# Pooled attention and a four-expert layer on one core: keys and values fetched as two accumulating half transfers

## The chip, the core and the metric

The kernel runs on one core of a Trainium2 chip. The core has a matrix engine (TensorE, in profiles PE, with its weight loads as PEld), three engines for element-wise work (VectorE = DVE, ScalarE = ACT, GpSimd = POOL), a queue engine (SyncE = SP), and 16 DMA engines that move data between the main memory and the on-chip memory. The metric is the device time of one execution in microseconds. The kernel before takes 524.53 us (median of three; 523.56 to 525.8).

## What is computed

Eight batches of eight heads, 576 queries of 64 numbers each. Keys and values are averaged over groups of 8 rows (72 pooled rows remain), then comes ordinary softmax attention, and its output passes through four experts, each two matrix products with a relu between, weighted per token.

```python
B, H, S, D = 8, 8, 576, 64; pool = 8
k_p = k.reshape(B, H, 72, 8, D).mean(axis=3)
v_p = v.reshape(B, H, 72, 8, D).mean(axis=3)
attn = softmax(q @ k_p.T / sqrt(D))
x = (attn @ v_p) as (4608, 512)
p = domain_probs / domain_probs.sum(-1)
for e in range(4):                     # w1[e]: 512x1024, w2[e]: 1024x512
    out += p[:, e] * (relu(x @ w1[e]) @ w2[e])
```

All inputs are float32 in main memory; GpSimd's transfers turn them into bfloat16 on their way.

## The kernel before

Work goes in chunks c of 512 tokens: c = 0 to 7 are the first 512 tokens of each batch, c = 8 the 64 last tokens of all batches together. A chunk has four steps, one for each expert e. In step (c, e), TensorE computes the first product of (c, e) and, mixed in, the second product of the step before; mixed in further is the attention of batch c + 1. The program places the small pieces by hand: each step has 16 numbered points, and `attention(c)` says at which pair of points of chunk c (n = 0 to 31) what is placed. The engines run their instructions in exactly this order.

The matrix products use a scheme with seven products of half-size blocks instead of eight. It needs sums and differences of blocks ("forms") of the weights and of the activations, made once for the weights:

```python
def combine_w1(e, engine=nc.vector):          # 4 operations 128x1024, bf16, in w1_bf
    ...
        lambda: add(out=w[:, S1], in0=w[:, A21], in1=w[:, A22]),
        ...                                   # S2, S4, S3
def combine_w2(e, engine=nc.vector):          # 4 operations 128x1024, into w2_t and w2_bf
    ...
def sums_of(c, e):                            # 4 operations 128x1024 of the activations (L701 to L704)
    ...
def relu_sum(out, ps, r):                     # VectorE drains a PSUM bank (L686)
    nc.vector._custom_dve(TENSOR_ADD_SAT, out=out, in0=ps[:], in1=r[:], s0=BIG, s1=0.0)
```

Where they are placed (`forms_due` is a queue from which each slot of a step takes one):

```python
if s == 1:
    forms_due.extend(nothing + combine_w1(2))         # nothing = four empty slots
elif s == 2:
    forms_due.extend(combine_w1(3))
elif s == 4:
    forms_due.extend(nothing[:2] + combine_w1(1) + combine_x(1))
elif s == 5:
    forms_due.extend(nothing[:3] + combine_w2(SPLIT[0]))
    forms_due.extend(combine_w2(SPLIT[1], nc.gpsimd) + combine_w1(0, nc.gpsimd))
```

Keys and values are loaded whole, 72 partitions of 8 heads x 8 rows x 64, and folded by VectorE: 8 rows to 4 (`first`), 4 to 2 and 2 to 1 (`rest`). Keys are written twice, side by side, and transposed by a DMA; values go to `vps` and are used as they are.

```python
def load_kv(b, src, nm):
    if b in (1, 2) and nm == "vraw":
        raw = w2_t[0:SP]...                            # borrowed room
    else:
        raw = rawpool.tile([SP, H, POOL, D], BF16, name="raw")[:]   # one buffer
    nc.gpsimd.dma_start(out=raw, in_=src[b].rearrange("h (j r) d -> j h r d", r=POOL))

def fold_parts(nm, b, hs, last):                       # hs: half of the heads
    def first():
        raw = raws[(nm, b)]
        nc.vector.tensor_add(out=raw[:, hs, 0:4, :], in0=raw[:, hs, 0:4, :], in1=raw[:, hs, 4:8, :])
    def rest():
        raw = raws[(nm, b)]
        nc.vector.tensor_add(out=raw[:, hs, 0:2, :], in0=raw[:, hs, 0:2, :], in1=raw[:, hs, 2:4, :])
        for out in last(hs):
            nc.vector.tensor_add(out=out, in0=raw[:, hs, 0, :], in1=raw[:, hs, 1, :])
    return [first, rest]

def loads_wait(b):                                     # GpSimd waits for the transposed keys
    nc.gpsimd.tensor_copy(out=mark[:], in_=state[("kpT", b)][0:1, 0, 0:1])
```

The order of the attention pieces in chunk c (b = c + 1):

```python
    if c == 1:
        keyed = 1
        add(0, lambda: queries(b))                     # DMA transpose of the queries
        for n, part in enumerate(key_parts(b)):
            add(n // 2, part)
    else:
        keyed = 1
        for n, part in enumerate(key_parts(b)[2:]):
            add(n, part)
    scored, valued, mixed = 7, 8 if c > 1 else 6, 11
    add(keyed, lambda: keys(b), lambda: loads_wait(b)) # DMA transpose of the keys; mark
    if c > 1:
        add(keyed + 1, lambda: load_v(b))
    if b + 1 < B:
        add(keyed + 1, lambda: (load_q(b + 1), load_q_rem(b + 1)))
    for pair in range(NPAIR):
        add(scored + pair, lambda pair=pair: scores(b, pair))
    for n, part in enumerate(value_parts(b)):
        add(valued + n, part)
    if b + 1 < B:
        add(valued + 4, lambda: queries(b + 1), lambda: load_k(b + 1))
        for n, part in enumerate(key_parts(b + 1)[:2]):
            add(30 + n, part)
    for r in range(NR):
        add(mixed + r, lambda r=r: context(b, r))      # attention x values on TensorE
        add(mixed + 1 + r, lambda r=r: turn(b, r))
```

In chunk 0 the plan `second_attention` does the same for batch 1, and issues keys, queries and values of batch 2 at its points 44, 51 and 66.

Of the kernel before, what the change touches and what calls it, by code (L numbers as in the profile page):

```python
# [11 lines left out]
ALU = mybir.AluOpType  # L12
AX = mybir.AxisListType
BF16 = mybir.dt.bfloat16
# [4 lines left out]
def kernel(  # L19
# [10 lines left out]
    nc = tc.nc  # L30
# [5 lines left out]
    POOL = 8  # L36
# [38 lines left out]
    w2_t = wpool.tile([P, len(SPLIT), 3, FCH // 2, TH], BF16, name="w2_t")  # L75
    h_s = wpool.tile([P, 3, FCH // 2, TH], BF16, name="h_s")

    raws = {}
    q_rems = {}

# [1 line left out]
    halves = [slice(i * H // 2, (i + 1) * H // 2) for i in range(2)]  # L82

    def load_kv(b, src, nm):
        if b in (1, 2) and nm == "vraw":
            raw = w2_t[0:SP].rearrange("p a b f d -> p (a b f d)")[:, 0:H * POOL * D].rearrange(
                "p (h r d) -> p h r d", h=H, r=POOL
            )
        else:
            raw = rawpool.tile([SP, H, POOL, D], BF16, name="raw")[:]  # L90
        nc.gpsimd.dma_start(
            out=raw, in_=src[b].rearrange("h (j r) d -> j h r d", r=POOL)
        )
        raws[(nm, b)] = raw

    def load_first(src, nm, hs):
        if nm not in raws:
# [34 lines left out]
    def load_k(b):  # L132
        load_kv(b, k, "kraw")

    def load_v(b):
        load_kv(b, v, "vraw")
# [57 lines left out]
    def fold_keys(b, hs):  # L194
        raw = raws[("kraw", b)]
        fold(raw, hs)
        for dup in range(2):
            nc.vector.tensor_add(out=kp[0:SP, hs, dup, :], in0=raw[:, hs, 0, :],
                                 in1=raw[:, hs, 1, :])

    def fold_parts(nm, b, hs, last):

        def first():
            raw = raws[(nm, b)]
            nc.vector.tensor_add(out=raw[:, hs, 0:4, :], in0=raw[:, hs, 0:4, :],  # L205
                                 in1=raw[:, hs, 4:8, :])

        def rest():
            raw = raws[(nm, b)]
            nc.vector.tensor_add(out=raw[:, hs, 0:2, :], in0=raw[:, hs, 0:2, :],  # L210
                                 in1=raw[:, hs, 2:4, :])
            for out in last(hs):
                nc.vector.tensor_add(out=out, in0=raw[:, hs, 0, :], in1=raw[:, hs, 1, :])

        return [first, rest]

    def key_parts(b):
        return [part for hs in halves for part in fold_parts(
            "kraw", b, hs, lambda hs: [kp[0:SP, hs, dup, :] for dup in range(2)])]
# [5 lines left out]
    def keys(b):  # L225
        state[("kpT", b)] = apool.tile([P, H, SPP], BF16, name="kpT", bufs=3)
        nc.sync.dma_start_transpose(
            out=state[("kpT", b)][:], in_=kp[:].rearrange("j h u d -> j (h u d)")
        )
# [13 lines left out]
    def queries(b):  # L243
        state[("qT", b)] = apool.tile([P, H, 2, P], BF16, name="qT", bufs=1)
        nc.sync.dma_start_transpose(
            out=state[("qT", b)][:].rearrange("c h r p -> c (h r) p"),
            in_=raws[("q", b)][:].rearrange("p h r d -> p (h r d)"),
        )
# [254 lines left out]
    def second_attention():  # L503

        lo, hi = halves

        return {
            42: [lambda: fold_keys(1, lo)],
            44: [lambda: fold_keys(1, hi), lambda: load_k(2)],
            47: [second_keys],  # L510
            50: [lambda: second_queries(0)],
            51: [lambda: second_queries(1), lambda: load_q(2), lambda: load_q_rem(2)],
            53: [lambda: scores(1, 0)],
            55: [lambda: scores(1, 1)],
            56: [lambda: fold_values(1, lo)],
            57: [lambda: scores(1, 2)],
            58: [lambda: fold_values(1, hi)],
            59: [lambda: scores(1, 3)],
            60: [lambda: context(1, 0), lambda: turn(1, 0)],
            61: [lambda: context(1, 1), lambda: turn(1, 1)],  # L520
            62: [lambda: context(1, 2), lambda: turn(1, 2)],
            63: [lambda: context(1, 3), lambda: turn(1, 3)],
            66: [lambda: load_v(2)],
        }

    def attention(c):

        lo, hi = halves
        b = c + 1
        plan = {}  # L530

        def add(n, *what):
            plan.setdefault(n, []).extend(what)

        if c % 2:
            i = c // 2
            add(18, lambda: rem_queries(i))
            add(23, lambda: rem_scores(i))
            add(26, lambda: rem_context(i))
            add(27, lambda: rem_turn(i))  # L540
        if b == B:
            for part in forms_of(B):
                add(31, part)
            return plan
        if c == 1:
            keyed = 1
            add(0, lambda: queries(b))
            for n, part in enumerate(key_parts(b)):
                add(n // 2, part)
        else:  # L550
            keyed = 1
            for n, part in enumerate(key_parts(b)[2:]):
                add(n, part)
        scored, valued, mixed = 7, 8 if c > 1 else 6, 11
        add(keyed, lambda: keys(b), lambda: loads_wait(b))
        if c > 1:
            add(keyed + 1, lambda: load_v(b))
        if b + 1 < B:
            add(keyed + 1, lambda: (load_q(b + 1), load_q_rem(b + 1)))
        for pair in range(NPAIR):  # L560
            add(scored + pair, lambda pair=pair: scores(b, pair))
        for n, part in enumerate(value_parts(b)):
            add(valued + n, part)
        if b + 1 < B:
            add(valued + 4, lambda: queries(b + 1), lambda: load_k(b + 1))
            for n, part in enumerate(key_parts(b + 1)[:2]):
                add(30 + n, part)
        for r in range(NR):
            add(mixed + r, lambda r=r: context(b, r))
            add(mixed + 1 + r, lambda r=r: turn(b, r))  # L570
        for n, part in enumerate(forms_of(b)):
            add((20, 21, 28, 29)[n], part)
        return plan
# [274 lines left out]
    with tc.manual_schedule(engines={ENG.PE, ENG.DVE, ENG.Activation, ENG.Pool, ENG.SP}):  # L848
# [52 lines left out]
        for s in range(len(steps) + 1):  # L901
            live = s < len(steps)
            if live:
                c, e = steps[s]
                if e == 0:
                    plan = second_attention() if c == 0 else {}
                    if 0 < c < B:
                        plan = {at + 2 * n + 1: what for n, what in attention(c).items()}
                    for n, what in plan.items():
                        placed.setdefault(n, []).extend(what)  # L910

            def between(j, n):
                point()
                if s > 0:
                    down(*steps[s - 1], j, n)
                slot()

            nothing = [lambda: None] * 4
            if s == 1:
                forms_due.extend(nothing + combine_w1(2))  # L920
            elif s == 2:
                forms_due.extend(combine_w1(3))
            elif s == 4:
                forms_due.extend(nothing[:2] + combine_w1(1) + combine_x(1))
            elif s == 5:
                forms_due.extend(nothing[:3] + combine_w2(SPLIT[0]))
                forms_due.extend(combine_w2(SPLIT[1], nc.gpsimd) + combine_w1(0, nc.gpsimd))
            for j in range(2):
                if not live:
                    for n in range(4):  # L930
                        between(j, n)
                elif s == 0:
                    for i in range(4):
                        up_half(j, i)
                        if j == 0 and i in (1, 2):
                            turn_here(0, i + 1)
                        if j == 0 and i == 2:
                            norm_probs()
                            for part in combine_x(0):
                                part()  # L940
                        between(j, i)
                elif s == 1:
                    for n in range(4):
                        between(j, n)
                    for n in range(4):
                        up_plain(c, e, [4 * j + n])
                elif s == E:
                    for n in range(4):
                        between(j, n)
                        if j:  # L950
                            up_plain(c, e, [2 * n, 2 * n + 1])
                elif splits(*steps[s - 1]):
                    up_down(c, e, j, *steps[s - 1])
                else:
                    up_seven(c, e, j, lambda n: between(j, n))
# [30 lines left out]
```

The softmax here doesn't subtract the row's maximum and nothing guards it: scores larger than these inputs give would overflow.

## Time and profile before

| | busy, us | share of 523.6 us |
|---|---|---|
| TensorE matmuls | 504.0 | 96% |
| TensorE weight loads | 363.5 | 69% |
| VectorE | 355.4 | 68% |
| ScalarE | 267.5 | 51% |
| GpSimd | 67.5 | 13% |
| DMA queue of GpSimd (inputs) | 22.63 MB | 31.0% of 16 engines |
| DMA queue of SyncE (output, transposes) | 18.29 MB | 18.7% of 16 engines |

The DMA engines are full for the first 70 us, when all weights come in, and on average about half busy or less afterwards (a share of 0.46 from 114 to 210 us). A matmul lasts longer than the distance between two of them (0.27 us against 0.11 us for 256 columns), so TensorE's busy share hides nothing but also says little; waits are read from the time between starts. In timeline lines the columns are start, duration, engine, source line, operation, what it writes and reads, count, and in brackets how long the engine was idle before it and what ended that. Two lines of transfers:

```profile
raw<-in_k_dram POOLq DMA_DIRECT2D x7, 576.0 KB, 11.4
raw<-in_v_dram POOLq DMA_DIRECT2D x5, 576.0 KB, 8.1
```

They give the count, the bytes as they arrive, and the median time from issue to landing.

### The profile page before, as it was taken

To read this page: it belongs to the slowest core of one execution; us is meant where nothing else is said; L and a number is where in the kernel's file an instruction comes from. 1 tells how busy PE (TensorE), PEld (TensorE's weight loads), DVE (VectorE), ACT (ScalarE), POOL (GpSimd) and SP (SyncE) were. 2 spreads that over 40 slices of the span, in tenths; PEclk is the share of its full clock that TensorE was granted. 3 is DMA by queue.
4 is the path that set the end of the run, shared out by engine and by line. 5 is a ranking of instruction groups with operands and counts; after the bars stand their busy time and mean duration, and the time that the engine had idled before them with its cause. 6 is when DMAs were issued, how large, how long until landed. Compare 5 with 4: busy or idle time off the path is not lost.

```text
span 523.6 us, 10155 instructions
## 1 busy us (share of the span) xinstructions
PE 504.0 (96%) x4171; PEld 363.5 (69%) x4171; DVE 355.4 (68%) x649; ACT 267.5 (51%) x467; POOL 67.5 (13%) x80
## 2 busy tenths in 40 slices
PE   8898989969999999999999999999999999999996
PEld 4745644558757876688668866886588768866883
DVE  2434787897857884878677876787677546764674
ACT  3653434636465545565465546653655446544650
POOL 8362102860020002000100020000000000000000
PEclk9999999999999999999999999999999999999999
DMA  9999999510199207920696059403510110011003
GB/s 133 207 206 206 199 149 179 107 30 1 24 169 107 25 0 142 145 36 11 106 143 65 2 94 157 70 11 57 94 32 0 41 52 1 11 42 40 1 1 80
DMA packets 75133, 41.56 MB, mean 79 GB/s; under 512 B 44480, under 2 KB 70464, under 8 KB 75088
## 3 DMA queue, kind: packets, MB, share of 16 engines
q0 software_dynamic: 33744, 22.63, 31.0%
q1 hardware_dynamic: 41344, 18.29, 18.7%
q8 instruction: 32, 0.52, 0.4%
q14 instruction: 13, 0.11, 0.1%
HBM read 45.16 MB, written 9.44 MB: 104 GB/s over the span
## 4 chain that ended last, share of the span: by engine, by line
PE 71%; DVE 13%; DMA 10%; POOL 2%; issue 2%; ACT 1%; POOLq 0%; ACTq 0%; SPq 0%; DVEq 0%
PE g_ps L638 30%; PE o_ps L817 19%; PE u_ps L755 16%; DMA w_bf<-in_moe_w_dram 5%; DMA raw<-in_v_dram 3%; DVE H_sb L686 3%; DVE acc L761 3%; DMA kpT<-kp 2%; PE h_ps L656 1%; PE two L262 1%; PE two L385 1%; POOL w_bf L142 1%; DVE h_s L701 1%; DVE x_tok L367 1%; DVE H_sb L702 1%
## 5 line engine op out<-in xcount | busy, mean ns | idle before, releaser
L638 PEld LDWEIGHTS <-w_bf 128*128 128x128 bf16 x1848 | 176.1, 98 | 49.5 <-issue 10.7
L817 PE MATMUL o_ps<-w_bf,H_sb 128*128 128x512 bf16 x640 | 161.5, 379 | 0.2 <-DMA w_bf<-in_moe_w_dram 0.2
L682 ACT COPY r<-g_ps 128x512 f32<-128x512 f32 x166 | 97.4, 586 | 106.3 <-PE g_ps L638 102.4
L638 PE MATMUL g_ps<-xf,w_bf 128*128 128x256 bf16 x1056 | 148.4, 272 | 2.8 <-DVE H_sb L686 1.8
L686 DVE CUSTOM_DVE_ANT_0 H_sb<-g_ps,r 128x512 bf16<-128x512 f32 x166 | 113.9, 687 | 48.1 <-ACT r L682 33.3
L761 DVE SCALAR_TENSOR_TENSOR acc<-u_ps,p_all,acc 128x512 f32<-128x512 f32 (+1 forms) x128 | 78.0, 612 | 43.8 <-ACT u_ps L781 43.1
L638 PE MATMUL g_ps<-xT,w_bf 128*128 128x256 bf16 x696 | 99.9, 273 | 2.0 <-DVE H_sb L686 2.0
L817 PEld LDWEIGHTS <-H_sb 128*128 128x128 bf16 x640 | 62.5, 98 | 46.1 <-issue 0.4
L689 ACT ACTIVATE H_sb<-g_ps 128x512 bf16<-128x512 f32 x98 | 58.4, 596 | 29.7 <-PE g_ps L638 29.7
L755 PEld LDWEIGHTS <-H_sb 128*128 128x128 bf16 x512 | 49.4, 98 | 8.2 <-DVE H_sb L702 2.4
L755 PE MATMUL u_ps<-w_bf,H_sb 128*128 128x256 bf16 x384 | 52.4, 273 | 1.1 <-DVE H_sb L702 0.9
L755 PEld LDWEIGHTS <-h_s 128*128 128x128 bf16 x384 | 37.5, 98 | 6.1 <-DVE h_s L703 1.8
L831 DVE SCALAR_TENSOR_TENSOR acc<-o_ps,p_all,acc 128x512 f32<-128x512 f32 x44 | 32.7, 746 | 11.3 <-PE o_ps L817 11.3
L755 PE MATMUL u_ps<-w_t,h_s 128*128 128x256 bf16 x256 | 38.4, 273 | 1.5 <-DVE h_s L703 1.5
L266 ACT ACTIVATE expT<-two 72x1024 bf16<-72x1024 f32 x28 | 28.6, 1020 | 13.4 <-PE two L262 13.4
L767 ACT COPY g_ps<-g_ps 128x512 f32<-128x512 f32 x32 | 18.3, 572 | 27.9 <-PE g_ps L638 27.9
L828 ACT ACTIVATE acc<-o_ps,p_all 128x512 f32<-128x512 f32 x36 | 24.8, 690 | 7.0 <-PE o_ps L817 7.0
L234 POOL COPY mark<-kpT 1x1 bf16<-1x1 bf16 x6 | 1.3, 218 | 205.9 <-DMA kpT<-kp 205.9
L781 ACT COPY u_ps<-u_ps 128x256 f32<-128x256 f32 x32 | 11.4, 357 | 26.7 <-PE u_ps L755 26.7
L205 DVE TENSOR_TENSOR raw<-raw 72x1024 bf16<-72x1024 bf16 x22 | 15.0, 681 | 13.5 <-DMA raw<-in_v_dram 13.5
L367 DVE TENSOR_TENSOR x_tok<-two,inv 128x512 bf16<-128x512 f32 x32 | 22.1, 691 | 1.1
L385 PEld LDWEIGHTS <-expT 72*128 72x128 bf16 x256 | 12.0, 98 | 12.4 <-DVE x_tok L367 4.8
(113 smaller groups left out, 377.2 us busy)
## 6 DMA issues: line engine op xcount, KB each, us to landing
out_dram<-acc SPq DMA_DIRECT2D x32, 256.0 KB, 2.9
w_bf<-in_moe_w_dram POOLq DMA_DIRECT2D x16, 256.0 KB, 9.7
w_bf<-in_moe_w_dram POOLq DMA_DIRECT2D x4, 1024.0 KB, 16.9
raw<-in_k_dram POOLq DMA_DIRECT2D x7, 576.0 KB, 11.4
q_sb<-in_q_dram POOLq DMA_DIRECT2D x7, 512.0 KB, 11.9
raw<-in_v_dram POOLq DMA_DIRECT2D x5, 576.0 KB, 8.1
w_t<-in_v_dram POOLq DMA_DIRECT2D x2, 576.0 KB, 13.2
out_dram<-acc SPq DMA_DIRECT2D x8, 128.0 KB, 2.3
```

The lines of the kernel that those rows point to most:

```text
L266: nc.scalar.activation(out=state[("expT", b)][:, 2 * pair:2 * pair + 2].rearrange("j h r s p -> j s (h r) p"), in_=two[0:SP].rearrange("j ...
L367: nc.vector.tensor_tensor(out=x_tok[:], in0=c_ps[:, :, :, 0:D], in1=inv[:].unsqueeze(3).to_broadcast([P, 2, NPAIR, D]), op=ALU.mult,)
L638: nc.tensor.matmul(bank[:, t, :], lhsT=w1_bf[:, e, block, kc, lo:lo + P], rhs=x[:, kc, :], start=(first and t == 0 and kc == 0), stop=(t = ...
L682: nc.scalar.copy(out=r[:], in_=ps[:])
L686: nc.vector._custom_dve(TENSOR_ADD_SAT, out=out, in0=ps[:], in1=r[:], s0=BIG, s1=0.0)
L689: nc.scalar.activation(out=out, in_=ps[:], func=ACT.Relu)
L755: nc.tensor.matmul(out, lhsT=lhs[0][:, lhs[1] + f, lhs[2]], rhs=rhs[0][:, rhs[1] + f, rhs[2]], start=(start and f == 0), stop=(f == FCH // ...
L761: nc.vector.scalar_tensor_tensor(out=acc, in0=ps, scalar=prob, in1=acc, op0=ALU.mult, op1=ALU.add,)
L767: nc.scalar.copy(out=s[:], in_=g[:])
L817: nc.tensor.matmul(sums[r][:], lhsT=hidden[(c, e)][:, fc, r * P:(r + 1) * P], rhs=w2_bf[:, e, fc, :], start=(fc == 0), stop=(fc == FCH - 1),)
L828: nc.scalar.activation(out=accs[(c, r)][:], in_=o_ps[:], func=ACT.Copy, scale=prob)
L831: nc.vector.scalar_tensor_tensor(out=dst, in0=o_ps[:], scalar=prob, in1=dst, op0=ALU.mult, op1=ALU.add,)
```

## The change

Keys and values of batches 2 to 7 come as two transfers each. The first brings rows 0 to 3 of every group of 8; the second brings rows 4 to 7 and adds them in flight to what the first wrote. VectorE's `first` is then not needed. Each goes to its own half of one buffer `raw_kv`, so keys and values can be fetched together; batch 1 is still fetched whole, over both halves. The second transfer must wait for the first. The order of pieces follows: in chunk c both halves of keys and values of batch c + 2 are issued at n = 17 and 19. For batch 2 the keys' halves are at points 44 and 47 of chunk 0 and the values' halves at 66. The forms of w1[3] come four slots later, and those of w1[0] go from GpSimd to VectorE. The aim is less work for VectorE and earlier loads.

```diff
+    raw_kv = rawpool.tile([SP, 2, H, POOL // 2, D], BF16, name="raw_kv")
...
+    def load_half(b, src, nm, half):
+        raws[(nm, b)] = raw_kv[:, 0 if nm == "kraw" else 1]
+        lo = half * POOL // 2
+        nc.gpsimd.dma_start(
+            out=raws[(nm, b)],
+            in_=src[b].rearrange("h (j r) d -> j h r d", r=POOL)[:, :, lo:lo + POOL // 2],
+            accum_op=ALU.add if half else ALU.bypass,
+        )
+    def load_later(b, half):
+        load_half(b, k, "kraw", half)
+        load_half(b, v, "vraw", half)
...
     def fold_parts(nm, b, hs, last):
-        def first():
-            ...
-        return [first, rest]
+        return [rest]
...                                                    # second_attention
-            44: [lambda: fold_keys(1, hi), lambda: load_k(2)],
-            47: [second_keys],
+            44: [lambda: fold_keys(1, hi), lambda: load_half(2, k, "kraw", 0)],
+            47: [second_keys, lambda: load_half(2, k, "kraw", 1)],
...
-            66: [lambda: load_v(2)],
+            66: [lambda: load_half(2, v, "vraw", 0), lambda: load_half(2, v, "vraw", 1)],
...                                                    # attention(c)
         if c == 1:
-            keyed = 1
-            add(0, lambda: queries(b))
-            for n, part in enumerate(key_parts(b)):
-                add(n // 2, part)
+            add(0, lambda: queries(b), *key_parts(b))
+            add(0, lambda: keys(b), lambda: loads_wait(b))
+            add(0, lambda: (load_q(b + 1), load_q_rem(b + 1)))
         else:
-            keyed = 1
-            for n, part in enumerate(key_parts(b)[2:]):
-                add(n, part)
-        scored, valued, mixed = 7, 8 if c > 1 else 6, 11
-        add(keyed, lambda: keys(b), lambda: loads_wait(b))
-        if c > 1:
-            add(keyed + 1, lambda: load_v(b))
-        if b + 1 < B:
-            add(keyed + 1, lambda: (load_q(b + 1), load_q_rem(b + 1)))
+            add(0, key_parts(b)[1], lambda: keys(b))
+        scored, valued, mixed = 7, 9, 11
...
         if b + 1 < B:
-            add(valued + 4, lambda: queries(b + 1), lambda: load_k(b + 1))
-            for n, part in enumerate(key_parts(b + 1)[:2]):
-                add(30 + n, part)
+            add(12, lambda: queries(b + 1))
+            add(17, lambda: load_later(b + 1, 0))
+            if b + 2 < B:
+                add(19, lambda: (load_q(b + 2), load_q_rem(b + 2)))
+            add(19, lambda: load_later(b + 1, 1))
+            add(30, key_parts(b + 1)[0])
...                                                    # steps
             elif s == 2:
-                forms_due.extend(combine_w1(3))
+                forms_due.extend(nothing + combine_w1(3))
             elif s == 4:
-                forms_due.extend(nothing[:2] + combine_w1(1) + combine_x(1))
+                w, x = combine_w1(0), combine_x(1)
+                forms_due.extend(w[:2] + combine_w1(1) + x[:1] + [lambda: (x[1](), w[2]())])
             elif s == 5:
-                forms_due.extend(nothing[:3] + combine_w2(SPLIT[0]))
-                forms_due.extend(combine_w2(SPLIT[1], nc.gpsimd) + combine_w1(0, nc.gpsimd))
+                forms_due.extend(w[3:] + combine_w2(SPLIT[0]))
+                for part in combine_w2(SPLIT[1], nc.gpsimd):
+                    part()
```

## The prediction

> **What bounds the kernel now.** I read the engine totals and the 40 slices first, then the busy time by stretches, then TensorE's timeline wherever a stretch shows it less than full, and last VectorE's and GpSimd's timelines in those places.
>
> ```profile
> PE 504.0 (96%) x4171; PEld 363.5 (69%) x4171; DVE 355.4 (68%) x649; ACT 267.5 (51%) x467; POOL 67.5 (13%) x80
> PE 71%; DVE 13%; DMA 10%; POOL 2%; issue 2%; ACT 1%; POOLq 0%; ACTq 0%; SPq 0%; DVEq 0%
> ```
>
> TensorE is the bound. From 114 to 523 us it is nearly gapless: a 128x256 matmul starts every 0.109 us (eight take 0.87 us in the chain), and one batch, counted between the score matmuls of successive batches (149.3, 203.0, 258.7, 312.4 us in the timeline), takes 53.7 us, or 54.7 with the remainder queries. VectorE is 68% busy on average, so taking work off it pays only where TensorE waits for it. Such places are few:
>
> ```profile
> 40.00:56.00 16.00, 13.30 (x90) 8.38 (x87) 9.74 (x20) 5.24 (x10) 3.12 (x4) 1.00 1.28 203
> 98.00:114.00 16.00, 11.22 (x97) 7.26 (x95) 15.83 (x20) 5.37 (x10) 15.05 (x7) 1.00 0.39 67
> 114.00:210.00 96.00, 95.74 (x816) 72.19 (x814) 69.87 (x130) 52.98 (x93) 6.11 (x9) 1.00 0.46 66
> ```
>
> The columns are busy time of PE, PEld, DVE, ACT and POOL. Between 98 and 114 us VectorE and GpSimd are both full and TensorE loses 4.8 us by this count. The timelines show the waits:
>
> ```profile
> 48.67 1.03 PE L638 MATMUL g_ps<-xT,w_bf 128*128 128x256 bf16 x8 [1.99 <-DVE H_sb L686]
> 109.36 1.03 PE L638 MATMUL g_ps<-xf,w_bf 128*128 128x256 bf16 x8 [1.77 <-DVE H_sb L686]
> 111.29 1.05 PE L755 MATMUL u_ps<-w_bf,H_sb 128*128 128x256 bf16 x8 [0.90 <-DVE H_sb L702]
> 113.82 0.61 PE L755 MATMUL u_ps<-w_t,h_s 128*128 128x256 bf16 x4 [1.48 <-DVE h_s L703]
> 212.63 0.29 PE L385 MATMUL two<-vp,expT 72*128 72x65 bf16 x4 [0.83 <-DVE vp L213]
> 376.19 0.29 PE L385 MATMUL two<-vp,expT 72*128 72x65 bf16 x4 [0.32 <-DVE vp L213]
> ```
>
> And what VectorE was doing there (first its wait at 46 us, then one operation beside GpSimd and the same one 15 us later without it):
>
> ```profile
> 46.13 0.69 DVE L586 TENSOR_TENSOR w_bf<-w_bf 128x1024 bf16<-128x1024 bf16 x1 [7.51 <-DMA w_bf<-in_moe_w_dram]
> 109.23 2.00 DVE L702 TENSOR_TENSOR H_sb<-H_sb 128x1024 bf16<-128x1024 bf16 x1
> 124.67 0.69 DVE L702 TENSOR_TENSOR H_sb<-H_sb 128x1024 bf16<-128x1024 bf16 x1
> 110.65 2.56 POOL L589 TENSOR_TENSOR w_bf<-w_bf 128x1024 bf16<-128x1024 bf16 x1
> ```
>
> So there are three separate losses. At 46 us the form sums of w1[3] stand in VectorE's queue ahead of evictions that TensorE needs, and their weights have not landed. From 93.7 to 113.2 us GpSimd runs eight 128x1024 sums, and VectorE's two-input operations take 1.2 to 2.6 us instead of 0.69. Twice later the values arrive late.
>
> [...] No transfer of the kernel before accumulates, so its cost is unmeasured here. [...]
>
> **The change, part by part.** TensorE, ScalarE and SyncE keep their instructions in the same order. VectorE's and GpSimd's change.
>
> *(a) VectorE's first folds.* The 22 operations of L205 (680 ns, 15.0 us in all) go. From 114 us on they lie beside a full TensorE, so this by itself is worth about nothing. Worth something is that keys and values of batches 3 to 7 now start a full half batch ahead: the transfers are placed at points 17 and 19 of 32 (32 points of 53.7 us are 1.7 us each, so 29 and 32 us into the batch), while keys are read at point 30 and values at point 9 of the next batch. Even two transfers in a row of some 8 us each fit. The two late-value waits go: 1.0 + 0.5 us of excess start-to-start time. **-1.5 us.**
>
> *(b) w1[3] four slots later.* Now two evictions, two merges and a third eviction come first, and the matmuls at 48.67 start at about 46.5: -2.1 us. Two checks: keys of batch 1 land at 48.4 (issued 33.57, 14.8 to landing), before their fold at about 49.2. Queries of batch 1 land at 36.32 + 20.5 = 56.8, and TensorE would want them at 58.67 - 2.3 = 56.4, so about 0.4 is given back. TensorE runs some **1.8 us** ahead from here to 95 us.
>
> *(c) GpSimd's eight sums become four*; the sums of w1[0] go to VectorE, four times 0.6 us, spread over 75 to 92 us, where the folds of batch 2 that go (four at 0.68, values moved later) more than make room. In the kernel before, start-to-start excess of TensorE over 98 to 114 us adds to 0.5 + 0.7 + 0.5 at the context matmuls and 1.9 + 1.1 + 1.6 at the end: 6.3 us that could go.
>
> *(d) The values of batch 2 arrive later.* Before, they were issued at 69.72 and landed 7.3 us later. Now they stand behind the mark that waits for batch 2's transposed keys, behind queries 3, and are two dependent transfers. Step by step:
> - Keys, first half: behind the weights still queued. Whole keys landed at 56.38 + 14.3 = 70.7; a half moves 36 packets per engine of 60 ns (the 512-byte ones) in place of 98 ns (1,024-byte), 1.4 us less: 69.3.
> - Keys, second half: issued 69.4. A whole transfer with an empty queue took 7.9 us (issue 145.22), so a half is about 6.5, plus an unknown cost of adding: 76. VectorE wants it at 75.8. Even.
> - Queries 2 are issued after it and land at about 79 (before: 73.2); their transposition at 79, that of the keys at 80.4, landing 2.8 later, so the mark is at about 83.2 (before: 83.14).
> - Queries 3 issue at 83.4, values' first half at 85.0. This is the place that keys 3 had (issued 85.2, landed after 10.8 us): 96.0 - 1.4 = 94.6.
> - Values' second half: issued 94.7, + 6.5 = **101.2**.
> - The fold of the first heads 0.7, one eviction 0.6, one w2 sum 0.6, the other heads 0.7: pooled values at 103.8.
>
> TensorE reaches the first context matmuls at 97.41 - 1.8 = 95.6 and waits until 103.8: **a new stall of about 8 us**. GpSimd's four sums (2.13 us each) start after that issue, 95 to 104, mostly while VectorE waits anyhow. From there to the next step's start the kernel before took 106.12 - 97.41 = 8.7 us, 1.7 of them waits: 7.0, and I add 0.3 for VectorE's backlog: 111.1. The comparable moment before: TensorE is past its last wait at 113.82, and has then done 28 matmuls of 0.109 us since 106.12, so without waits it would have stood at 110.8. **(b), (c) and (d) together: +0.3 us.** The gain of 1.8 + 6.3 is eaten by the wait for one transfer.
>
> Sum: -1.5 + 0.3 = -1.2, and +0.3 as my allowance for a slow clock after a long stall. 524.5 - 0.9, rounded: **523.5 us**.
>
> **The rivals.**
> - *Values in time.* If adding costs nothing and the queue drains 3 to 5 us sooner, values land at 96.5 and the stall is 3 to 4 us: about 518. If they never matter, all of 1.8 + 6.3 + 1.5 comes: 515. For it: GpSimd's share in the critical stretch does halve. Against: each link of (d) has its duration in this profile.
> - *Adding is slow.* If an accumulating packet takes two or three times a plain one (+2 to 4 us each, twice in the chain of (d)), values land at 105 to 109 and the stall outlasts 10 us, and the clock may drop: 528 to 532. The steady batches have 18 us of room and would not feel it. Only above 10 us more per transfer would every batch wait, and that alone passes 2%.
> - *VectorE freed, so everything faster.* 15 us of folds go, 3% of the span. Against it: from 114 us on TensorE has its matmuls back to back, and the profile gives no place where that time could come off.
>
> **Range and chances.** The first rival sets the lower end (I take 517.5), the second the upper (530). 2% is 10.5 us; faster by that needs more than every wait I could find: 4%. Slower by that needs adding to be slow enough for all batches: 5%. Within 2%: 91%.
>
> **What would show it.** Right: no wait at 46 to 48 us; GpSimd's sums end near 104 instead of 113; VectorE waits at the value fold of batch 2 near 92 to 101 for the accumulating transfer and TensorE for the pooled values; batches of 53.7 and 54.7 us later without the late-value waits. Wrong: the second half landing in 3 us or in 15, TensorE passing 95 to 105 us without a stall, or a slower batch after 150 us.

## The result and the profile after

The changed kernel takes 532.89 us (median; 530.56 to 533.83) beside 524.94 for the kernel before on the same chip: a ratio of 1.0147, 95% interval 1.0105 to 1.019. So it is about 8 us slower. It was predicted at 523.5 us, with a range of 517.5 to 530. The profiled executions last 530.5 and 523.6 us.

The engine totals of the changed kernel:

```profile
PE 502.8 (95%) x4125; PEld 364.3 (69%) x4171; DVE 342.7 (65%) x629; ACT 267.5 (50%) x467; POOL 73.2 (14%) x83
```

VectorE has lost 12.7 us of work, as intended, and TensorE's own work is the same (46 records of matmuls are missing from this trace; the weight loads are all there). Yet the span is longer. The totals cannot say why. The stretches can (columns as before: start and end, length, busy time of PE, PEld, DVE, ACT, POOL, granted clock, DMA share, GB/s):

```profile
40.00:56.00 16.00, 15.34 (x107) 10.09 (x108) 10.82 (x21) 7.03 (x12) 3.96 (x5) 1.00 1.28 203
77.00:81.00 4.00, 1.93 (x9) 0.69 (x7) 3.97 (x10) 0.00 (x0) 0.00 (x0) 1.00 1.41 144
81.00:84.00 3.00, 0.52 (x2) 0.28 (x3) 1.75 (x3) 0.00 (x0) 0.00 (x0) 0.80 1.28 200
84.00:92.00 8.00, 8.00 (x34) 3.36 (x33) 1.51 (x3) 2.98 (x5) 2.59 (x4) 0.86 0.92 167
98.00:104.00 6.00, 4.48 (x30) 2.18 (x29) 3.52 (x1) 4.39 (x7) 5.92 (x4) 1.00 0.77 74
104.00:110.00 6.00, 0.51 (x7) 0.40 (x8) 5.82 (x7) 0.00 (x0) 4.65 (x3) 0.72 0.35 70
114.00:210.00 96.00, 95.32 (x821) 73.73 (x828) 68.67 (x129) 51.65 (x93) 10.54 (x10) 1.00 0.59 75
```

The hole at 46 us is gone (15.34 busy against 13.30). From 114 us on TensorE is as full as before (95.32 of 96 us, before 95.74). Between them are two holes, one at 78 to 84 us and one at 102 to 108 us, each followed by a lower granted clock. TensorE's timeline names what ended each wait:

```profile
83.48 3.21 PE L656 MATMUL h_ps<-xT,w_bf 128*128 128x512 bf16 x8 [4.55 <-DMA xT<-x_tok]
108.04 0.40 PE L390 MATMUL two<-vp,expT 72*128 72x65 bf16 x4 [5.50 <-DVE vp L218]
109.89 0.38 PE L390 MATMUL two<-vp,expT 72*128 72x65 bf16 x4 [1.45 <-DVE vp L218]
```

The second is the stall that was predicted. The first is new: TensorE waits for a transposition of batch 1's attention output, which the change does not touch.

Both kernels have the same 4,171 weight loads on TensorE in the same order, so the distance between the nth one of one trace and of the other shows where time is lost. The first column is the time in the kernel before, the others how much later (+) or earlier (-) the changed kernel is there:

| at, us | predicted | measured | what lies before it |
|---|---|---|---|
| 50 | -2.1 | -1.9 | forms of w1[3] later |
| 92 | -1.8 | **+5.0** | first stall |
| 100 | +6.4 | +13.8 | second stall |
| 115 | +0.3 | +8.3 | fewer sums on GpSimd |
| end | -1.2 | +6.85 | two late-value waits gone |

From row to row the prediction has -2.1, +0.3, +8.2, -6.1, -1.5; measured are -1.9, **+6.9**, +8.8, -5.4, -1.5. Only the second row shows a large difference. Of its 6.9 us some 0.8 are lost ahead of the stall, where TensorE waits 0.75 us at 57.6 us for the queries of batch 1 (0.4 was foreseen); the stall and the slower clock behind it make about 6.

That the third row agrees (8.8 for 8.2) is luck. TensorE reaches the second stall at 102.5 us, where 95.6 was predicted, and the pooled values are ready at 109.8, where 103.8 was predicted: both ends are 6 to 7 us late. In e1 below, where the first stall is gone, the same row is 11.0 us.

How the first stall comes about is read from GpSimd's timeline, which issues all these transfers in program order, and SyncE's, which issues the transpositions:

```profile
69.04 1.42 POOL L96 DMA_DIRECT2D raw_kv<-in_k_dram  x1 [16.59 <-DMA raw_kv<-in_k_dram]
69.91 1.47 POOL L118 DMA_DIRECT2D q_sb<-in_q_dram  x1
86.65 0.18 POOL L239 COPY mark<-kpT 1x1 bf16<-1x1 bf16 x1 [14.57 <-DMA kpT<-kp]
88.73 0.84 POOL L96 DMA_DIRECT2D raw_kv<-in_v_dram  x1
97.40 1.41 POOL L96 DMA_DIRECT2D raw_kv<-in_v_dram  x1 [7.83 <-DMA raw_kv<-in_v_dram]
98.27 2.69 POOL L626 TENSOR_TENSOR w_t<-w_bf 128x1024 bf16<-128x1024 bf16 x1
```

```profile
70.97 7.81 SPq L411 DMA_TRANSPOSE xT<-x_tok  x4
81.32 1.82 SPq L250 DMA_TRANSPOSE qT<-q_sb  x1
83.18 1.78 SPq L232 DMA_TRANSPOSE kpT<-kp  x1
```

GpSimd waits 16.59 us for the keys' first half, and the queries of batch 2 wait behind it: issued at 69.91, in the kernel before at 60.97. From 67.9 to 71.0 us no packet of GpSimd's queue starts: the DMA engines have run dry. Then they have everything to do at once, just as the four transpositions of batch 1's output start. Two stretches of the kernel before, and the first of them in the changed kernel (the second stands above):

```profile
66.00:71.00 5.00, 4.87 (x42) 2.82 (x41) 3.79 (x8) 3.43 (x5) 0.85 (x1) 1.00 1.17 138
77.00:81.00 4.00, 4.00 (x20) 1.84 (x19) 3.86 (x11) 0.10 (x1) 0.00 (x0) 1.00 1.00 189
```

```profile
66.00:71.00 5.00, 4.20 (x34) 2.25 (x33) 3.83 (x9) 2.76 (x4) 1.96 (x3) 1.00 0.10 14
```

The DMA share at 66 to 71 us falls from 1.17 to 0.10, and at 77 to 81 us it rises from 1.00 to 1.41 while TensorE's busy time falls from 4.00 to 1.93. So in the kernel before the DMA engines are full at 77 to 81 us too, and not only in the first 70: with the transpositions alone, as the next table shows. The packet records of the trace, counted per microsecond, show what the transpositions then get (GpSimd's packets of 512 or 1,024 bytes, SyncE's of 256 bytes, which are transpositions; other sizes left out):

```
us        before: GpSimd  SyncE   after: GpSimd  SyncE   e1: GpSimd  SyncE
75               136      1              178     27             14    611
76                30    597              225     53              0    719
77                 0    937              169    118              0    512
78                 0    380              197    212              0    377
79                 0    771              183    231              0    827
81                 0    752                0    554              0    645
82                 0    309                0    883              0      7
```

In the microseconds that they fill with nothing beside them, the transpositions run at about 720 to 940 packets. Beside GpSimd's transfers they get 27 to 231, and in the kernel before a single one at 75 us, beside its values; there TensorE does not wait for them yet. The counts show no fixed share between the two queues: with GpSimd's packets of 128 bytes, which the table leaves out, the changed kernel has 212 beside 216 at 78 us, but 231 beside 350 at 79 us, and 27 beside 178 at 75. That plain transfers hold up transpositions is what the runs below test. The time from issue to landing of the four transpositions, before and after:

```profile
DMA to landing us min/median/max: 2.5/4.1/5.5
```

```profile
DMA to landing us min/median/max: 5.8/7.6/10.2
```

The second stall is read from VectorE's timeline. The first heads' values are folded by two operations, which the prediction counted with 0.7 us (the first line is a form ahead of them):

```profile
97.84 3.68 DVE L626 TENSOR_TENSOR w_t<-w_bf 128x1024 bf16<-128x1024 bf16 x1
104.11 1.74 DVE L215 TENSOR_TENSOR raw_kv<-raw_kv 72x512 bf16<-72x512 bf16 x1 [2.60 <-DMA raw_kv<-in_v_dram]
105.89 2.09 DVE L218 TENSOR_TENSOR vp<-raw_kv 72x256 bf16<-72x256 bf16 x1
```

The fold takes 3.8 us, because GpSimd's sums (98.27 to 107.8) run beside it; right after them operations of the same kind take their ordinary time (109.10 and 109.55: 0.41 and 0.29 us).

### The profile page after: what moved, and what is told of

The parts are those of the page before. It is cut to its first block, busy times and chain, and to the rows that moved or that the text cites. A ratio compares the mean times of both kernels' runs of the same rounds, so it can differ in the third digit from the quotient of the medians.

```text
span 530.5 us, 10085 instructions
## 1 busy us (share of the span) xinstructions
PE 502.8 (95%) x4125; PEld 364.3 (69%) x4171; DVE 342.7 (65%) x629; ACT 267.5 (50%) x467; POOL 73.2 (14%) x83
## 4 chain that ended last, share of the span: by engine, by line
PE 77%; issue 8%; DVE 7%; DMA 4%; POOL 2%; ACT 1%; POOLq 0%; ACTq 0%; DVEq 0%
PE g_ps L638 33%; PE o_ps L817 22%; PE u_ps L755 17%; DMA raw_kv<-in_v_dram 3%; DVE acc L761 2%; DMA H_sb<-in_v_dram 1%; PE h_ps L656 1%; PE two L267 1%; DVE H_sb L686 1%; PE two L390 1%; PE h_ps L669 1%; DVE h_s L701 1%; DVE xf L602 1%; DVE vp L218 0%; ACT g_ps L767 0%
## 5 line engine op out<-in xcount | busy, mean ns | idle before, releaser
L817 PE MATMUL o_ps<-w_bf,H_sb 128*128 128x512 bf16 x598 | 154.7, 380 | 2.2
L638 PE MATMUL g_ps<-xT,w_bf 128*128 128x256 bf16 x696 | 100.7, 274 | 0.0
L96 POOL DMA_DIRECT2D raw_kv<-in_k_dram x12 | 13.7, 1145 | 113.1 <-DVE kp L218 91.0
L96 POOL DMA_DIRECT2D raw_kv<-in_v_dram x12 | 15.2, 1267 | 84.0 <-DVE vp L218 67.1
```

The lines of the kernel that those rows point to most:

```text
L96: nc.gpsimd.dma_start(out=raws[(nm, b)], in_=src[b].rearrange("h (j r) d -> j h r d", r=POOL)[:, :, lo:lo + POOL // 2], accum_op=ALU.add i ...
L638: nc.tensor.matmul(bank[:, t, :], lhsT=w1_bf[:, e, block, kc, lo:lo + P], rhs=x[:, kc, :], start=(first and t == 0 and kc == 0), stop=(t = ...
L817: nc.tensor.matmul(sums[r][:], lhsT=hidden[(c, e)][:, fc, r * P:(r + 1) * P], rhs=w2_bf[:, e, fc, :], start=(fc == 0), stop=(fc == FCH - 1),)
```

## The experiments

The theory: the loss belongs to batch 2 alone. (i) Queries 2 behind the keys' second half collide with the transpositions: the first stall. (ii) The values of batch 2 come late: the second stall. (iii) GpSimd's sums, which run beside the fold, lengthen it. Rivals: adding in flight is slow and costs in every batch, or the moved forms are to blame. "End" is the shift of the last weight load against the kernel before (+6.85 for the changed kernel); ratios are to the kernel before, run on the same chip. One trace stands for each "end", and ends are good to about 1.3 us: the traces of e2, e5 and e8 have 3.4 us of half clock at about 19 us, ahead of all that is argued here, and their shift at 50 us is -0.7 to -1.0 where the others have -1.8 to -2.5. Where it matters, the medians of the times decide.

### e1: queries of batch 2 first

```diff
-            47: [second_keys, lambda: load_half(2, k, "kraw", 1)],
-            51: [lambda: second_queries(1), lambda: load_q(2), lambda: load_q_rem(2)],
+            47: [second_keys],
+            51: [lambda: second_queries(1), lambda: load_q(2), lambda: load_q_rem(2),
+                 lambda: load_half(2, k, "kraw", 1)],
```

> The changed kernel, but queries of batch 2 are issued ahead of the keys' second half. Transfer order (my theory): the plain transfers of queries 2 are over before 71 us, so the transposes of batch 1's attention output are no longer held up; the 4.9 us stall of TensorE at 78.6 us and the half clock after it go, the mark comes near 83 us in place of 86.7, the values' second half lands near 100 in place of 104; about 526 to 528 us. Slow adding: the transfers that add are as slow as before, 532 to 533. Moved sums (VectorE overloaded by the forms of w1): no change, 532 to 533.

Measured: 528.84 us, ratio 1.0065 [1.0041, 1.0089], end +2.95. Queries 2 are issued at 59.16, and the transpositions land in 2.5 to 6.2 us. TensorE's waits and VectorE's fold:

```profile
78.62 1.89 PE L657 MATMUL h_ps<-xT,w_bf 128*128 128x512 bf16 x8 [0.42 <-DMA xT<-x_tok]
103.97 0.40 PE L390 MATMUL two<-vp,expT 72*128 72x65 bf16 x4 [7.62 <-DVE vp L218]
```

```profile
100.46 1.33 DVE L215 TENSOR_TENSOR raw_kv<-raw_kv 72x512 bf16<-72x512 bf16 x1 [8.12 <-DMA raw_kv<-in_v_dram]
101.82 2.09 DVE L218 TENSOR_TENSOR vp<-raw_kv 72x256 bf16<-72x256 bf16 x1
```

The first stall goes from 4.55 to 0.42 us, and the shift at 92 us is -1.2 where it was +5.0. That settles (i). Only 3.9 us of it reach the end: TensorE now arrives earlier at the second stall and waits longer there (7.62 against 5.50), although the values too land earlier (100.5 against 104.1). The prediction had queries 2 the other way round, but it had no first stall either: its 101.2 for the landing then fits the measured 100.5; its 0.7 us for the fold, where 3.4 are measured, does not. The time is just above the 526 to 528 that I expected.

The eight matmuls of L656 or L657 also show the clock. After 0.42 us of idling they take 1.89 us; after 4.55 us of idling, in the changed kernel, 3.21. There the granted clock is 0.50 from 82.8 to 86.2 us, which makes the 0.80 and 0.86 of the two stretches above. In e4 below they take 1.89 us after a wait of 2.03; in e10 the clock is halved from 98.4 to 105.2 us around waits of 2.27 and 1.45 us.

### e2: batch 2 whole, as before

```diff
-            44: [..., lambda: load_half(2, k, "kraw", 0)],
-            47: [second_keys, lambda: load_half(2, k, "kraw", 1)],
-            66: [lambda: load_half(2, v, "vraw", 0), lambda: load_half(2, v, "vraw", 1)],
+            44: [..., lambda: load_k(2)],
+            47: [second_keys],
+            66: [lambda: load_v(2)],
     # batch 2 has its first folds again; GpSimd's sums wait for the slots, as before
```

> The changed kernel, but keys and values of batch 2 come whole and are folded by VectorE as in the kernel before; batches 3 to 7 still come as two halves with adding, and the forms stay moved. Transfer order: both stalls belong to batch 2, so they go; what stays are the gains: 518 to 521 us. Slow adding: ten of the twelve adding transfers are still there, so most of the loss stays: 529 to 532. Moved sums: 531 to 533.

Measured: 520.14 us, ratio 0.9896 [0.9875, 0.9917], end -4.99. Batches 3 to 7 still use the adding halves. All of the loss has gone, and more than the kernel before is gained. Neither adding in the later batches nor the moved forms costs anything; it is batch 2's transfers, together with the place of GpSimd's sums, which this run puts back too.

### e4: second halves overwrite in place of adding

```diff
-            accum_op=ALU.add if half else ALU.bypass,
+            accum_op=ALU.bypass,
```

This leaves out rows 0 to 3 of every group of 8 from the pooled keys and values of batches 2 to 7; transfers and their order stay.

> The changed kernel, but the second half overwrites the first in place of adding (four of eight rows are left out of each mean). All waits and transfers stay. Transfer order: the adding itself costs next to nothing, 531 to 533 us. Slow adding: the loss goes, 520 to 525. Moved sums: 532 to 533.

Measured: 528.72 us, ratio 1.006 [1.0035, 1.0084], end +3.10. I had expected hardly a change from the changed kernel, so adding is dearer than I thought. The keys' second half lands 5.2 us after its issue without adding and 7.0 with it; the record of the issue is 0.83 us long without and 1.42 with it (the next instruction starts after 0.83 and 0.87), and the median packet of 512 bytes takes 60 and 84 ns. Queries 2 land at 78.0 in place of 81.2, the stall at 80 us falls from 4.55 to 2.03, and the mark stands at 83.36 where it was 86.65. The shift at 92 us is +0.3: of the 6.2 us that e1 gains there, 4.6 go with the adding alone. Adding is thus the larger part of the first stall, but only because it lengthens a queue that stands in the wrong place: in e1 it is there, and the stall is not. And without adding queries 2 land earlier than the predicted 79, yet TensorE still waits 2.03 us for the transpositions. The fold still takes 3.9 us here, from 100.4 on.

### e5: the moved forms alone

```diff
     # the kernel before, whole transfers and first folds, with
-                forms_due.extend(combine_w1(3))                       # s == 2
+                forms_due.extend(nothing + combine_w1(3))
     # and w1[0]'s four sums on VectorE, as in the change; w2[2]'s stay on GpSimd
```

> The kernel before with only the forms moved (those of w1[3] four slots later, those of w1[0] on VectorE). Transfer order: this part is the gain, 1.8 us at 46 us and 2 to 5 us of the 6 us of stalls between 98 and 114: 518 to 521 us. Moved sums: 528 to 533. Slow adding says nothing of it.

Measured: 520.43 us, ratio 0.9904 [0.9877, 0.9931], end -5.06. With e2 (-4.99) this says that in sum the moved forms bring all that the change brings. The halves of batches 3 to 7 do take away the two late-value waits: from 115 us to the end e2 gains 1.5 us and e5 0.4. But from 92 to 115 us e2 gains only 3.1 us and e5 4.3, so nothing of it is left.

### e6: values early

```diff
     # on top of e1
+            65: [lambda: load_half(2, v, "vraw", 0)],                 # ahead of the mark
-            66: [lambda: load_half(2, v, "vraw", 0), lambda: load_half(2, v, "vraw", 1)],
     # and the values' second half right behind the mark, ahead of queries 3
```

> The changed kernel with queries 2 ahead of the keys' second half, and in addition the values' first half of batch 2 issued before the mark and the second half directly behind it, ahead of queries 3. Transfer order: the second half is issued at about 83 us and lands near 90, before VectorE wants it at about 91, so no wait of TensorE is left between 70 and 105 us beyond 1 us; all gains of the change stay: 516 to 519 us, faster than both kernels. Slow adding: each transfer that adds still takes its extra time, 524 to 528.

Measured: 523.12 us, ratio 0.993 [0.9897, 0.9963], end -2.22. The second stall shrinks to 0.90 us, which supports (ii). I had expected 516 to 519 us. But now the values' first half is issued at 70.26 beside the transpositions, and the first stall is back, with another plain transfer than in the changed kernel:

```profile
82.09 2.86 PE L657 MATMUL h_ps<-xT,w_bf 128*128 128x512 bf16 x8 [3.72 <-DMA xT<-x_tok]
102.53 0.29 PE L390 MATMUL two<-vp,expT 72*128 72x65 bf16 x4 [0.90 <-DVE vp L218]
```

So it does not matter whether queries or values stand there; both are plain transfers.

### e7: GpSimd's sums wait for the pooled values

```diff
-                for part in combine_w2(SPLIT[1], nc.gpsimd):
-                    part()
+                # GpSimd first copies one number of vps[2], then runs the four sums, one per slot
```

> The changed kernel, but GpSimd starts its four sums for w2[2] only when the pooled values of batch 2 are written (it copies one number of them first). [...]

Measured: 530.31 us, ratio 1.008 [1.0046, 1.0113], end +5.59. I had expected 530 to 532 us, by an estimate from the traces: the fold of the first heads in 0.7 us in place of 3.8, so a second stall 3 us shorter, and about 1 us of it given back behind; and 532.5 to 534 if the sums have no part in that stall. With no sums beside it the fold has its ordinary time, and the pooled values are ready at 106.8 in place of 109.8. The sums then lie beside other work of VectorE (first line the fold, second a sum of activations that takes 0.69 us when alone), and much is given back:

```profile
104.21 0.42 DVE L215 TENSOR_TENSOR raw_kv<-raw_kv 72x512 bf16<-72x512 bf16 x1 [5.19 <-DMA raw_kv<-in_v_dram]
...
116.65 1.84 DVE L701 TENSOR_TENSOR h_s<-H_sb 128x1024 bf16<-128x1024 bf16 x1
```

### e8, e9, e10: batch 2's transfers clear of the four transpositions

```diff
     # on top of e1; the values' halves leave point 66
-            add(0, lambda: keys(b), lambda: loads_wait(b))
+            add(0, lambda: keys(b), lambda: nc.gpsimd.tensor_copy(
+                out=mark[:], in_=state[("xT", c)][0:1, KC - 1, NT - 1:NT]))  # last transposition
+            add(0, lambda: load_half(b, v, "vraw", 0), lambda: loads_wait(b))
+            add(0, lambda: load_half(b, v, "vraw", 1))
+            add(0, *combine_w2(SPLIT[1], nc.gpsimd))        # e9: after queries 3, as in the change
```

> The changed kernel with queries 2 ahead of the keys' second half; the values' first half of batch 2 waits for the last transpose of batch 1's attention output and goes before the mark, its second half right behind the mark; then GpSimd's four sums, then queries 3. Transfer order: no transfer runs beside the transposes at 72 to 78 us, so the first stall is 1 us or less; the values land near 91, before the fold; the sums run from 84 to 93, where VectorE has room. Left are the gains: 515 to 518 us, faster than the kernel before by 1.2 to 1.8%. If the loss came from the adding or from the moved sums, it stays: 524 or more.

> As the run before it (batch 2 in order), but queries 3 ahead of GpSimd's sums, as in the changed kernel. The sums run some 3 us later and meet the value fold: 0 to 3 us slower than that run, 516 to 520.

> Batch 2 in order, but the second halves overwrite in place of adding (four of eight rows are left out of each mean). Transfer order: the adding is hidden once nothing waits for it, so the same time within 1 us. Slow adding: 3 us faster or more.

Measured: e8 524.91 us, ratio 0.999 [0.9978, 1.0002]; e9 525.08, ratio 0.9992 [0.9979, 1.0005]; e10, which like e4 leaves rows 0 to 3 out, 522.59, ratio 0.9948 [0.9928, 0.9967]. I had expected e8 and e9 to beat both kernels (515 to 518 and 516 to 520 us), and they only equal the kernel before. Both stalls are as they should be as far as transfers go: no wait at 78 us, and no wait of VectorE for the values. But TensorE waits, and VectorE's timeline ahead of the fold shows for what:

```profile
88.02 2.58 DVE L606 TENSOR_TENSOR xf<-xT 128x512 bf16<-128x512 bf16 x1
90.52 2.34 DVE L606 TENSOR_TENSOR xf<-xT,xf 128x512 bf16<-128x512 bf16 x1
92.78 2.60 DVE L592 TENSOR_TENSOR w_bf<-w_bf 128x1024 bf16<-128x1024 bf16 x1
95.31 2.61 DVE L593 TENSOR_TENSOR w_bf<-w_bf 128x1024 bf16<-128x1024 bf16 x1
...
99.04 0.41 DVE L215 TENSOR_TENSOR raw_kv<-raw_kv 72x512 bf16<-72x512 bf16 x1
```

```profile
99.83 0.30 PE L390 MATMUL two<-vp,expT 72*128 72x65 bf16 x4 [2.94 <-DVE vp L218]
```

Four operations that take 0.41 to 0.69 us alone take 10.1 us beside GpSimd's four sums (87.64 to 97.4). I had expected e10 within 1 us of e8, but taking the adding out brings 2.3 us: with it, GpSimd's issues and the mark come 0.7 us later. The values' first half now lies beside the transposition of the keys, which lands in 7.3 us where it took 3.9 in e1. So the mark stands at 86.19, hardly earlier than the 86.65 of the changed kernel: this order clears the four transpositions, not that one.

### e11, e12, e13: the sums of w2[2] on VectorE

```diff
     # e11: on top of e8; e12: on top of the changed kernel; e13: on top of e5
-                four sums of w2[SPLIT[1]] on GpSimd
-                forms_due.extend(w[3:] + combine_w2(SPLIT[0]))
+                forms_due.extend(w[3:] + combine_w2(SPLIT[0]) + combine_w2(SPLIT[1]))
     # e13 has whole transfers, and its queue ends with combine_w2(SPLIT[1]) likewise
```

> Batch 2 in the order that keeps its transfers clear of the transposes, and no sums on GpSimd at all: the four of w2[2] stand in VectorE's queue of forms behind those of w2[1]. [...] If VectorE simply has too much to do between 86 and 100 us, or the adding transfer of values still holds the fold, TensorE still waits 3 to 5 us near 100 us and the time is 523 to 525.

> The changed kernel, with only the four sums of w2[2] moved from GpSimd to VectorE, as the last of its forms. Transfers are as in the changed kernel, so the stall at 78 us stays (5 us of idling) and the values' second half lands at about 104. If contention was 3 us of the second stall, the fold of the first heads takes 0.7 us instead of 3.8, pooled values are ready at 106.5 to 107, nothing is given back behind it, and the time is 528 to 530. If the landing alone sets the stall, the time stays at 532 to 533.

> The kernel before with the forms moved as in the change and all its sums on VectorE: whole transfers, first folds, nothing on GpSimd but transfers and marks. If the transfers by halves are worth about nothing at their best, it is within 1 us of the version that has them in the better order with the sums on VectorE, both 515 to 519. If adding in flight does pay once its order is right, this one is 2 us or more slower than that one.

Measured: e11 518.87 us, ratio 0.9867 [0.9846, 0.9888], end -6.56; e12 528.68, ratio 1.0061 [1.004, 1.0083], end +2.88; e13 519.99, ratio 0.9886 [0.9865, 0.9907], end -6.12. For e11 I had expected 515 to 518 us, with VectorE's sums at 0.6 to 0.7 us again and less than 1 us of waiting for pooled values, if it was GpSimd's sums that held e8 up. The same stretch of VectorE in e11 as above in e8, and the wait of TensorE:

```profile
88.04 0.68 DVE L591 TENSOR_TENSOR w_bf<-w_bf 128x1024 bf16<-128x1024 bf16 x1
...
94.75 0.42 DVE L215 TENSOR_TENSOR raw_kv<-raw_kv 72x512 bf16<-72x512 bf16 x1 [2.45 <-DMA raw_kv<-in_v_dram]
```

```profile
97.41 0.29 PE L390 MATMUL two<-vp,expT 72*128 72x65 bf16 x4 [0.97 <-DVE vp L218]
```

Between e8 and e11 only the four sums change engine (queries 3 are issued earlier for it), and the medians go from 524.91 to 518.87, some 6 us. That settles that GpSimd's sums cost it; by what way they slow VectorE, no run shows.

The 6 us are not all waiting. e8 waits 2.94 and 1.55 us for pooled values, e11 0.97: 3.5 us less. And from 100.7 to 107.6 us the clock of e8 is halved; in e11 it is not. The same eight matmuls in e8 and in e11:

```profile
101.88 1.89 PE L642 MATMUL g_ps<-xT,w_bf 128*128 128x256 bf16 x8
```

```profile
97.54 1.04 PE L641 MATMUL g_ps<-xT,w_bf 128*128 128x256 bf16 x8
```

Counted over the weight loads of that stretch, the half clock costs e8 an estimated 2.4 us. Waits and clock together make the 6 us.

e11 beats both kernels, the one before by 1.3% and the changed one, by the two ratios, by 2.8%; its median misses my 515 to 518 by 0.9 us, for 0.97 us of waiting remain at the values. In e12 the first stall stays (3.56 us of waiting), the values land at 102.7, and the fold has its ordinary time:

```profile
102.71 0.42 DVE L215 TENSOR_TENSOR raw_kv<-raw_kv 72x512 bf16<-72x512 bf16 x1 [4.03 <-DMA raw_kv<-in_v_dram]
103.16 0.29 DVE L218 TENSOR_TENSOR vp<-raw_kv 72x256 bf16<-72x256 bf16 x1
```

Its end is 4.0 us better than that of the changed kernel, of which about 1.4 us is an earlier landing that the edit does not explain. e13 has no adding at all and comes within 1.1 us of e11 (I had expected 1), with overlapping intervals: in the best order tried, adding in flight is worth 1 us or nothing.

## Why the prediction was wrong

**(a) First folds and late values: right.** VectorE's busy time falls by 12.7 us, the net of the folds that go, the sums of w1[0] that come and what GpSimd slows, and no time comes of it from 114 us on. The two late-value waits are gone: -1.0 and -0.5 us by the shift, -1.5 predicted. The starts that the prediction lists make a batch with remainder queries 55.7 us and not 54.7; that holds the first of these waits, and without it the changed kernel takes 54.7.

**(b) Forms of w1[3]: right as far as it goes.** -1.9 us at 50 us, -2.1 predicted; the other traces with these forms have -0.7 to -2.5. But the sentence "TensorE runs some 1.8 us ahead from here to 95 us" failed: it is 5.0 us behind by 92.

**(c) Fewer sums on GpSimd: right in sign.** 5.4 us come back between 100 and 115 us, 6.1 in my working. The forms alone (e5) make 5.1 us by the end.

**(d) Values of batch 2: the failing step.** Its terms, one by one:

| term | predicted | measured |
|---|---|---|
| keys, second half issued, landed | 69.4, 76 | 69.0, 76.0 |
| queries 2 landed | 79 | 81.2 |
| mark | 83.2 | 86.65 |
| values, first half issued, second half issued | 85.0, 94.7 | 88.7, 97.4 |
| second half, issue to landing | 6.5 | 6.7 |
| landing to first heads folded | 0.7 | 3.8 |
| pooled values ready | 103.8 | 109.8 |

The step that failed is "Queries 2 are issued after it and land at about 79". I followed them only to the keys' mark, where nothing seemed lost (83.2 against 83.14). I did not ask what else uses the DMA engines from 70 to 80 us: the transpositions of batch 1's output, for which TensorE waits from 78.9. The overlap that I left out is the first stall, about 6 us; e1 takes it away, and e6 brings it back with another transfer. The landing time as such is not the mistake: in e4 it is 78.0, and part of the stall stays. Two things of (d) go with it: the transpositions of queries and keys stand behind it, and the mark is 3.4 us late.

The second step that failed is "mostly while VectorE waits anyhow", said of GpSimd's four sums. I had the slowing in my own text, with 2.00 against 0.69 us, and did not apply it to the fold that stands behind that wait. The fold took 3.8 us for 0.7; in e7 the time from landing to pooled values is 3 us shorter, and e8 and e11 show the same slowing over a longer stretch.

**The rivals.** "Adding is slow" was partly right: an adding packet takes some 1.4 times a plain one, not the two or three times of that rival, but in this order, through the first stall above all, it is worth 4 us (e4). Its time of 528 to 532 was nearest, its place was not: values landed at 104.1, before its 105 to 109, and the loss that was not foreseen lay 20 us earlier. The 0.3 us for a slow clock was an allowance of mine, and no run shows it. What the runs show is more: the granted clock is 0.72 at 104 to 110 us and 0.56 at 110 to 114 us. The half clock costs an estimated 1.3 us behind the first stall (3.21 less 1.89 for the eight matmuls) and 1.2 behind the second (counted over the weight loads, without the waits).

What stays open is how the DMA engines divide their time between the queues: no run isolates it. Open too is what brings the half clock: it came with e10's waits of 2.27 and 1.45 us, and not with e4's single one of 2.03 (granted clock 1.00 from 81 to 92 us). A version of e1 with the sums on VectorE was not tried.

## What to carry to other kernels

When a transfer is split in two that depend on each other, everything behind the second in the issuing engine's program waits for the first to land (16.59 us here); ask what those others collide with when they come late, above all transpositions for which the matrix engine waits. Keep big plain transfers clear of such transpositions (27 to 231 packets per microsecond beside them here, for 720 to 940 alone), by order or by a wait on the last of them, and look which transposition they meet next. And sums on GpSimd are not free because VectorE is waiting: they cost where the work behind that wait is on the path (a fold of 3.8 us here, 0.7 without them).

## What was not expected of the hardware

- Transpositions by DMA fall from about 720 to 940 packets per microsecond to 27 to 231 beside GpSimd's transfers, and their landing goes from 2.5 to 5.5 us to 5.8 to 10.2.
- The keys' second half of 288 KB lands in 7.0 us when it adds and in 5.2 when it does not; the median 512-byte packet takes 84 ns against 60.
- TensorE's clock was halved for 6.8 us around waits of 2.27 and 1.45 us (e10); eight 128x256 matmuls took 1.90 us there, 1.04 at full clock.
- Under four sums of GpSimd in a row, VectorE's sums of 0.41 to 0.69 us took 2.3 to 2.6 us, and once 3.68.
